# Two fp32 transformer layers on one core: the output-bias column joins the tile of two scalars

## The chip, the cores and the metric

The kernel runs on one core of a Trainium2 chip. The number given is device time in microseconds of one launch, the median of several runs; a profiled execution adds a trace of the engines: PE (TensorE matmuls, with PEld for the loads of their stationary operand), DVE (VectorE), ACT (ScalarE), POOL (GpSimd) and SP (SyncE, which issues nearly all DMAs).

## The reference

One sequence of 2048 rows of width 640 goes through two layers, each a linear-attention block (32 heads of 20) and a squared-ReLU block (hidden width 1728). Both layers use the same weights.

```python
def _A_ref(x, wqkv, wo):                       # linear attention
    q, k, v = split_heads(x @ wqkv)
    phi = lambda t: jnp.where(t > 0, t + 1, jnp.exp(t)) + 1e-6
    pq, pk = phi(q), phi(k)
    kv = einsum("bhsd,bhse->bhde", pk, v)
    den = einsum("bhqd,bhd->bhq", pq, pk.sum over s) + 1e-6
    return (einsum("bhqd,bhde->bhqe", pq, kv) / den) merged @ wo

def _B_ref(x, w1, b1, w2, b2):                 # squared ReLU
    h = x @ w1 + b1
    r = where(h > 0, h, 0)
    return (r * r) @ w2 + b2

x = x + _A_ref(_layernorm(x), A_wqkv, A_wo)    # layer 1
x = x + _B_ref(_layernorm(x), B_w1, B_b1, B_w2, B_b2)
x = x + _A_ref(_layernorm(x), A_wqkv, A_wo)    # layer 2, the same weights
x = x + _B_ref(_layernorm(x), B_w1, B_b1, B_w2, B_b2)
```

## The kernel before

All products are fp32 in three passes: each operand is held as a high and a low half in the matmul format (`R32`), and high x low, low x high and high x high add up in PSUM. The rows are cut into 16 tiles of 128; four of them make a group (`TG`, `GT` = 512 columns).

**The attention half of a layer**, first pass. Tile by tile the rows are normalized, turned and split into `xT`; `part` (its matmuls are at line 574) multiplies them with the weights `kq`, 512, 256 or 320 columns at a time, to give phi(k) and phi(q). The row tiles (`xh`) and phi(k) (`kh`), split, are multiplied into the matrix `G` by `g_part`, also through line 574, 512 columns at a time, three matmuls for each of five PSUM banks. From `G`, the value weights and `wo` a matrix `M` (tiles `uM`) is made for each layer.

**The second half**, group by group: phi(q), divided by its denominator, times `M` (lines 574 and 595), normalization, and then the squared-ReLU block. Its first product is done partly by a Strassen scheme, with 256 columns per matmul (line 1510) and 512 in its rests (line 1520), partly plainly (line 1476, 512 columns). The hidden tiles `h` are split and go into the second product at line 1659 (`fc2_tile`), 512 columns per matmul: for four row tiles the stationary operand is a piece of `h` and the moving one a weight unit `u`, and for the fifth accumulator, the strip of the last 128 output columns, the weight is stationary and `h` moves. The weight units are kept split in DRAM and come back through seven buffers: six of the pool `tmp` (tag `u`, `RING`) and a seventh of the pool of the second half (`ring_tile`, also named `u`). The seventh exists for this half only.

A planner inside the kernel (`Clock`) chooses the order of this half from a table of costs at build time; the recorded order is then fixed, and engines wait for each other by semaphores.

**Where tiles lie.** A tile is a range of bytes in each of the 128 partitions of SBUF. Pools on the left are laid out one after the other from the start, each tile rounded up to 32 bytes: `cpool` (the constants), `small`, `tmp`, and then the pools of a half (`a_` with `G`, `GT`, `acc`, `r`, later `m_` with `uM`). Pools on the right (`ax_` with `xh` and `kh`, later `b_` with `x1`, the seventh `u`, `h` and `hr`) are laid out back from the end.

**The constants around the change.** `scalars` holds -0.5 and 1.0 for each partition; the layer norms raise to the power -0.5 with it (line 530) and one copy makes a tile of ones (line 733). `b2col` holds the last 128 output biases, one per partition. `late_consts` loads it with one DMA of 0.5 KB early in the first pass (line 275), and six copies (line 1668) spread it over a PSUM bank before the strips of the groups.

Of the kernel before, what the change touches and what calls it, by code (L numbers as in the profile page):

```python
# [8 lines left out]
F32 = mybir.dt.float32  # L9
# [4 lines left out]
P = 128  # L14
# [212 lines left out]
def kernel(  # L227
# [15 lines left out]
    cpool = ctx.enter_context(tc.tile_pool(name="cpool", bufs=1))  # L243
# [16 lines left out]

    ident = cpool.tile([P, P], F32, name="ident")
    make_identity(nc, ident)
    scalars = cpool.tile([P, 2], F32, name="scalars")
    neghalf, one = scalars[:, 0:1], scalars[:, 1:2]
    nc.vector.memset(one, 1.0)
    nc.vector.memset(neghalf, -0.5)
    b2bc = cpool.tile([P, D], F32, name="b2bc")
    b2col = cpool.tile([P, 1], F32, name="b2col")
    b1sb = cpool.tile([P, NF], F32, name="b1sb")

    def late_consts():
# [2046 lines left out]
```

## Time and profile before

| | us |
|---|---|
| median of 3 runs | 1376.81 |
| lowest and highest run | 1375.03, 1379.39 |
| the profiled execution | 1382.9 |
| its span, first to last instruction | 1381.2 |

The profiled execution is 6.1 us above the median of the runs, and 1.7 us of it lie outside its span. The mean granted TensorE clock in the span is 0.994 of full speed.

In the views below, a row of the chain of work gives when a piece starts, how long it lasts, the engine, the tile written and the line, and how many instructions make it up. Rows of groups give line, engine, operation, tiles, shape and count, then busy time and mean ns of one, then the idle time before them. Matmuls overlap each other in the pipeline, so the mean time of one is longer than the time from one start to the next; a piece of the chain divided by its count gives the latter.

### The profile page before, as it was taken

How to read it: one execution, taken by the hardware profiler on the slowest of the kernel's cores; microseconds unless marked ns; L12 is line 12 of the kernel's file. 1: busy time of each engine (PE TensorE's matmuls, PEld its weight loads, DVE VectorE, ACT ScalarE, POOL GpSimd, SP SyncE). 2: the span in 40 equal slices, each digit the busy share in tenths (PEclk: the TensorE clock that was granted, in tenths of full speed). 3: DMA queues.
4: the chain of work that ended last, by engine and by line, in shares of the span. 5: the costliest groups of instructions: out<-in, count | busy, mean ns of one | idle time of the engine just before them, and what ended most of it. 6: DMA issues, size and time to landing. Idle time of an engine off the chain costs nothing.

```text
span 1381.2 us, 21322 instructions
## 1 busy us (share of the span) xinstructions
PE 1337.4 (97%) x7616; PEld 1180.7 (85%) x7616; DVE 982.9 (71%) x1928; ACT 770.5 (56%) x1753; POOL 147.2 (11%) x196
## 2 busy tenths in 40 slices
PE   9999989989999999999999999999899999999999
PEld 8888879878888879888888889997788888898887
DVE  8888968887887787354256678799788876874323
ACT  5888845646664655446336687565365644554421
POOL 2334310000000000000012232100000000000000
PEclk9999999999999999999999999999999999999999
DMA  6679685397779768698731114166877788587684
GB/s 200 226 267 333 245 274 181 123 350 240 250 248 307 282 201 307 239 375 306 266 127 44 58 39 132 52 193 229 304 242 221 253 303 265 184 298 273 229 313 175
DMA packets 120240, 316.11 MB, mean 229 GB/s; under 512 B 15110, under 2 KB 40326, under 8 KB 119462
## 3 DMA queue, kind: packets, MB, share of 16 engines
q1 hardware_dynamic: 118622, 312.06, 65.4%
q10 hardware_dynamic: 1512, 2.69, 0.7%
q8 instruction: 60, 0.98, 0.3%
q14 instruction: 46, 0.38, 0.1%
HBM read 251.28 MB, written 64.85 MB: 229 GB/s over the span
## 4 chain that ended last, share of the span: by engine, by line
PE 71%; DMA 12%; DVE 11%; issue 2%; SPq 2%; ACT 1%; POOL 1%; ACTq 0%; DVEq 0%; POOLq 0%
PE PS L574 25%; PE PS L1659 21%; PE PS L1510 15%; PE PS L1520 4%; DMA pqt<-pq 4%; DMA u<-kept_wH 2%; PE PS L1476 2%; DMA u<-kept_w 2%; DMA u<-kept_wG 1%; SPq L773 1%; DMA u<-kept_wE 1%; PE PS L1188 1%; DVE bn L524 1%; DVE uprep L407 1%; PE PS L927 1%
## 5 line engine op out<-in xcount | busy, mean ns | idle before, releaser
L1659 PE MATMUL PS<-u,h 128*128 128x512 f32 x1318 | 346.1, 397 | 1.4 <-ACT s L1532 0.7
L562 ACT ACTIVATE z<-y 32x160 f32<-32x160 f32 x767 | 256.1, 334 | 88.4 <-DVE y L549 69.3
L574 PE MATMUL PS<-kq,xT 128*128 128x320 f32 (+2 forms) x1575 | 283.4, 334 | 4.3 <-DVE r L686 3.5
L1659 PEld LDWEIGHTS PS<-u,h 128*128 128x128 f32 x1318 | 241.1, 190 | 50.3 <-DMA u<-kept_w 1.0
L574 PEld LDWEIGHTS PS<-kq,xT 128*128 128x128 f32 x1575 | 250.0, 188 | 31.5 <-DVE r L686 3.8
L1510 PE MATMUL PS<-tx,u 128*128 128x256 f32 x1152 | 162.7, 284 | 11.1 <-DMA u<-kept_wH 5.9
L1510 PEld LDWEIGHTS PS<-tx,u 128*128 128x128 f32 x1152 | 151.4, 192 | 16.9 <-DMA u<-kept_wH 6.5
L1588 ACT ACTIVATE hr<-PS,b1sb 128x512 f32<-128x512 f32 x104 | 71.2, 685 | 140.9 <-PE PS L1520 123.2
L1510 PEld LDWEIGHTS PS<-xTb,u 128*128 128x128 f32 x864 | 120.5, 189 | 20.1 <-DVE PS L1552 6.8
L1510 PE MATMUL PS<-xTb,u 128*128 128x256 f32 x864 | 127.4, 283 | 7.2 <-DVE PS L1552 4.6
L574 PE MATMUL PS<-kh,xh 128*128 128x512 f32 x480 | 126.9, 398 | 0.0
L529 POOL TENSOR_SCALAR rs<-mv 128x1 f32<-128x1 f32 x62 | 30.5, 492 | 831.0 <-DVE mv L526 831.0
L574 PEld LDWEIGHTS PS<-kh,xh 128*128 128x128 f32 x480 | 88.1, 190 | 15.7
L1594 DVE TENSOR_TENSOR hr<-hr 128x512 f32<-128x512 f32 x71 | 48.7, 687 | 73.6 <-ACT h L1607 73.3
L677 ACT ACTIVATE e<-PS 128x320 f32<-128x320 f32 (+4 forms) x128 | 53.2, 434 | 83.5 <-PE PS L574 71.1
L1607 ACT ACTIVATE h<-hr 128x512 fp32r<-128x512 f32 x104 | 65.0, 629 | 62.3 <-PE PS L1659 61.0
L1659 PE MATMUL PS<-h,u 128*128 128x512 f32 x328 | 94.0, 395 | 0.0
L1597 DVE TENSOR_TENSOR h<-hr,h 128x512 fp32r<-128x512 f32 x104 | 70.9, 685 | 11.4 <-ACT hr L1592 7.4
L685 DVE TENSOR_SCALAR e<-e 128x320 f32<-128x320 f32 (+4 forms) x128 | 41.5, 325 | 50.8 <-ACT e L677 50.3
L1520 PE MATMUL PS<-xTb,u 128*128 128x512 f32 x288 | 76.1, 394 | 0.0
L1659 PEld LDWEIGHTS PS<-h,u 128*128 128x128 f32 x328 | 59.9, 188 | 12.3
L864 POOL TENSOR_TENSOR acc<-acc,r 128x640 f32<-128x640 f32 x28 | 50.7, 1810 | 176.8 <-DVE r L686 176.8
(178 smaller groups left out, 1889.6 us busy)
## 6 DMA issues: line engine op xcount, KB each, us to landing
u<-kept_w SPq DMA_DIRECT2D x116, 640.0 KB, 5.5
u<-kept_wE SPq DMA_DIRECT2D x48, 512.0 KB, 4.3
u<-kept_wH SPq DMA_DIRECT2D x48, 512.0 KB, 5.1
u<-kept_wG SPq DMA_DIRECT2D x48, 512.0 KB, 5.3
u<-kept_wF SPq DMA_DIRECT2D x48, 512.0 KB, 5.2
x<-x SPq DMA_DIRECT2D x48, 320.0 KB, 5.6
pqt<-pq SPq DMA_DIRECT2D x128, 80.0 KB, 5.3
x<-xr SPq DMA_DIRECT2D x32, 320.0 KB, 3.6
```

The costliest lines, as they stand in the source:

```text
L562: nc.scalar.activation(d, v, AF.Copy)
L574: nc.tensor.matmul(ps, a, b, start=first and i == 0, stop=last and i == 2)
L677: nc.scalar.activation(self.e[:, a:b], ps, AF.Exp)
L685: nc.vector.tensor_scalar(e, e, 1.0, PHI_EPS, op0=ALU.min, op1=ALU.add)
L864: nc.gpsimd.tensor_tensor(out=acc, in0=acc, in1=r, op=ALU.add)
L1510: nc.tensor.matmul(ps, l[:, d], r[:, d], start=start and d == 0 and n == 0, stop=d == 1 and n == 2, skip_group_check=True,)
L1520: nc.tensor.matmul(ps, l[:, k], r, start=False, stop=n == 2, skip_group_check=True)
L1588: nc.scalar.activation(r, ps, AF.Relu, bias=b1sb[:, c : c + 1])
L1594: nc.vector.tensor_tensor(out=r, in0=r, in1=r, op=ALU.mult)
L1597: nc.vector.tensor_tensor(out=h[:, 1], in0=r, in1=h[:, 0].bitcast(F32), op=ALU.subtract)
L1607: yield "ACT", cost("ACT", GT), lambda: nc.scalar.activation(h[:, 0], r, AF.Square)
L1659: nc.tensor.matmul(ps, l, r, start=(first or new) and k == 0, stop=end and k == len(a) - 1, **loose)
```

## The change

`b2col` is no longer a tile of its own. The tile `scalars` gets a third column, and the DMA of line 275 writes into that column. A tile of 8 or of 12 bytes takes the same 32, so nothing moves up to `b2bc`; behind it the 32 bytes of `b2col` are gone, and every later tile of the left pools starts 32 bytes nearer to the start of its partition. The right pools stay where they were. The engines' instructions, their order and their waits are the same in both built programs; only addresses differ.

The start bytes in the two built programs, and what is left of them when divided by 64:

| tile (pool) | before | after | by 64, before | by 64, after |
|---|---|---|---|---|
| `ident`, `scalars`, `b2bc` (`cpool`) | 1152, 1664, 1696 | same | 0, 0, 32 | same |
| `b2col` | 4256 | 1672, in `scalars` | 32 | 8 |
| `b1sb` (`cpool`) | 4288 | 4256 | 0 | 32 |
| 12 tiles of tag `f`: `xt`, `st`, `y`, `z`, `pqt`, `xr` and others (`tmp`) | from 5376 | from 5344 | 0 | 32 |
| 2 tiles of tag `T`: `xT`, `xTb` (`tmp`) | 36096, 56576 | 36064, 56544 | 0 | 32 |
| 5 tiles of tag `w`: `kq`, later `tx`, `uT`, `uS` (`tmp`) | from 77056 | from 77024 | 0 | 32 |
| 6 weight units of tag `u` (`tmp`) | from 128256 | from 128224 | 0 | 32 |
| `G`, `uM` (`a_`, `m_`) | from 159616 | from 159584 | 0 | 32 |
| 3 tiles of tag `r`: phi(k), phi(q) (`a_`) | from 175968 | from 175936 | 32 | 0 |
| 8 tiles of tag `x`: `xh`, `kh` (`ax_`) | from 188384 | same | 32 | 32 |
| `x1`, the seventh `u`, `h`, `hr` (`b_`) | 185312, 205792, from 210912, from 223200 | same | 32 | 32 |

The tiles of `tmp` start at a multiple of 256 before and 224 past one after; so do `x1`, the seventh `u`, `xh`, `kh` and `h` in both.

```diff
@@ -260,12 +260,11 @@
 
     ident = cpool.tile([P, P], F32, name="ident")
     make_identity(nc, ident)
-    scalars = cpool.tile([P, 2], F32, name="scalars")
-    neghalf, one = scalars[:, 0:1], scalars[:, 1:2]
+    scalars = cpool.tile([P, 3], F32, name="scalars")
+    neghalf, one, b2col = (scalars[:, i:i + 1] for i in range(3))
     nc.vector.memset(one, 1.0)
     nc.vector.memset(neghalf, -0.5)
     b2bc = cpool.tile([P, D], F32, name="b2bc")
-    b2col = cpool.tile([P, 1], F32, name="b2col")
     b1sb = cpool.tile([P, NF], F32, name="b1sb")
 
     def late_consts():
```

## The prediction

> **What bounds the kernel now.** I read the page's busy times and its chain first, then a table by stage, then the matmuls by shape, and last the chain piece by piece at places where equal matmuls read differently placed tiles. The first two:
>
> ```profile
> PE 1337.4 (97%) x7616; PEld 1180.7 (85%) x7616; DVE 982.9 (71%) x1928; ACT 770.5 (56%) x1753; POOL 147.2 (11%) x196
> ...
> q1 hardware_dynamic: 118622, 312.06, 65.4%
> ...
> PE 71%; DMA 12%; DVE 11%; issue 2%; SPq 2%; ACT 1%; POOL 1%; ACTq 0%; DVEq 0%; POOLq 0%
> ```
>
> TensorE is busy nearly throughout and carries 71% of the chain that ended last; DMA and DVE carry most of the rest. By stage (the middle row is the first pass of layer 2, the rows above and below it the squared-ReLU half of layers 1 and 2, each cut in two; columns: us, busy time and count of PE, PEld, DVE, ACT and POOL, granted clock, DMA share, GB/s):
>
> ```profile
> 262.00:480.00 218.00, 209.51 (x1205) 184.68 (x1205) 176.20 (x350) 121.00 (x264) 8.94 (x16) 0.98 0.79 271
> 480.00:700.00 220.00, 214.58 (x1199) 186.41 (x1198) 114.97 (x223) 104.98 (x238) 7.12 (x17) 0.99 0.78 277
> 700.00:882.00 182.00, 182.00 (x972) 159.63 (x971) 131.40 (x256) 120.14 (x299) 45.79 (x44) 1.00 0.24 74
> 941.00:1160.00 219.00, 207.67 (x1195) 181.66 (x1196) 173.09 (x347) 116.10 (x254) 7.71 (x16) 0.99 0.77 262
> 1160.00:1381.20 221.20, 214.23 (x1213) 186.64 (x1211) 110.86 (x214) 87.46 (x188) 3.55 (x8) 1.00 0.70 250
> ```
>
> From 700 to 882 us PE never stops: there a nanosecond per matmul is a nanosecond of the kernel. In the four other stretches PE stands still 5 to 11 us each, so most, but not all, of a change on PE arrives at the end.
>
> **The change, part by part.** No instruction is added, removed or moved, and no wait either. The column's DMA (0.5 KB, issued at 10.5 us) and its six copies stay; only the byte they touch is another, and it is read 397 us and later. I cost them at nothing:
>
> ```profile
> L1668 ACT ACTIVATE PS<-b2col x6: 594/597/600, 396.9 to 1290.9; 128x512 f32<-128x512 f32 x6
> L275 SPq DMA_DIRECT2D b2col<-in_B_b_dram x1: 328/328/328, 10.5 to 10.5; - x1
> ```
>
> What is left is where tiles lie. I write 0 and 32 for the remainder of a start byte by 64. Before, `tmp` is at 0, and `h`, `kh`, `xh` and the seventh weight buffer at 32; after, all of them are at 32. So the trace of before holds both cases, and the question for each engine is whether its operations cost more or less by it.
>
> *TensorE.* The matmuls that move 512 columns:
>
> ```profile
> L1659 PE MATMUL PS<-u,h 128*128 128x512 f32 x1306 | 344.5, 398 | 1.4 <-ACT s L1532 0.7 <-DMA u<-kept_w 0.7
> L574 PE MATMUL PS<-kq,xT 128*128 128x512 f32 x570 | 136.7, 391 | 0.2 <-DVE GT L716 0.2
> L574 PE MATMUL PS<-kh,xh 128*128 128x512 f32 x480 | 126.9, 398 | 0.0
> L1659 PE MATMUL PS<-h,u 128*128 128x512 f32 x328 | 94.0, 395 | 0.0
> L1520 PE MATMUL PS<-xTb,u 128*128 128x512 f32 x288 | 76.1, 394 | 0.0
> L1476 PE MATMUL PS<-xTb,u 128*128 128x512 f32 x200 | 48.3, 392 | 1.7 <-ACT xTb L286 1.7
> ```
>
> Equal shapes, and yet 391 to 398 ns. By the addresses of the built program, 1,445 of these 3,172 matmuls have one operand at 0 and the other at 32 (I call them mixed): 1,384 of line 1659, where `h` at 32 meets one of the six units at 0, and 36 and 25 of lines 1520 and 1476, where `xTb` at 0 meets the seventh unit. After the change none is mixed. Pieces of the chain show what that is worth. Uniform ones:
>
> ```profile
> 16.68 3.42 PE PS L574 x15
> 352.63 2.05 PE PS L1659 x9
> 382.75 3.42 PE PS L1476 x15
> 1270.07 1.39 PE PS L1520 x6
> 1274.26 2.28 PE PS L1476 x10
> ```
>
> and mixed ones:
>
> ```profile
> 355.36 4.89 PE PS L1659 x21
> 1271.46 2.80 PE PS L1659 x12
> 1276.54 3.50 PE PS L1659 x15
> 1280.03 3.50 PE PS L1476 x15
> ```
>
> Line 1476 is the cleanest pair: 15 matmuls of one kind take 3.42 us (228.0 ns each) where the unit is in a buffer at 0, and 3.50 (233.3) where it is in the seventh. Line 1659 shows it the other way round: with its unit in the seventh buffer, at 32 like `h`, nine take 2.05 (227.8); otherwise 12 take 2.80, 15 take 3.50 and 21 take 4.89 (232.9 to 233.3). So it is not the buffer; it is whether the two operands agree. Nor is it the clock or the load of the DMA engines, for the slower piece had less of the latter (us, PE busy and matmuls touched, clock, DMA share, GB/s):
>
> ```profile
> 1274.26:1276.54 2.28, 2.28 (x11) 1.00 1.01 351
> 1280.03:1283.53 3.50, 3.50 (x16) 1.00 0.57 198
> ```
>
> A uniform run isn't at its best from the start: six that follow 256-column matmuls take 1.39 us, 231.7 each. In the 15 of 3.42 the other nine then take 2.03, 225.6; with the nine of 2.05 beside it (227.8) I take 226.7 once settled. A run of n was 233.3n when mixed and becomes 6 x 231.7 + 226.7(n - 6): 10 ns less for 6, 29 for 9, 49 for 12, 69 for 15. The pieces of this stage hold 6 to 21, most 6 to 12; I take 10, which is 3.6 ns per matmul. The terms:
>
> - 1,445 mixed x 3.6 ns = 5.2 us.
> - 502 uniform ones of lines 1520 and 1659 (252 and 250) stand between mixed ones and rarely settle; 1.5 ns each, 0.8 us.
> - 480 `kh`,`xh` matmuls come in threes and sixes between `kq`,`xT` runs, so the operands agree inside but change over at both ends; they last 398 ns against 391. I take half of these 7 ns: 1.7 us.
> - 570 `kq`,`xT` matmuls meet the same change-over once in 15: about 0.7 ns, 0.4 us.
>
> Sum 8.1 us. The bounds: 2.3 if every run is as short as 6 and nothing else gains (1,445 x 1.6), and 15 if all settle at once (1,445 x 6.6, 502 x 5.0, 480 x 7).
>
> How much arrives: from 700 to 882 all of it. Outside, the chain is on PE for (0.71 x 1381 - 182) / 1199 = 67% of the time; where it is on a DMA, that DMA often waited for a buffer which PE frees, so more than 67% passes. I take 80% of 8.1 = 6.5 us. What is late next is a weight load or the turned phi(q), as at the DMA's 12% today.
>
> The Trainium skill says otherwise ("SBUF — State Buffer", section "A bandwidth-pool intuition that's wrong (but worth ruling out)"): loads of the stationary operand have a second, independent read port, so an engine's two reads shouldn't meet. By that rule the sum would be 0; the pieces of line 1476 above speak against it at 512 columns.
>
> *DVE and ACT.* Splits of 128x512 that read and write tiles at 0, and the same on `h` and `hr` at 32:
>
> ```profile
> L1429 DVE TENSOR_TENSOR tx<-tv,tx 128x512 fp32r<-128x512 f32 x16 | 11.0, 686 | 4.6 <-ACT tx L1427 4.6
> L1597 DVE TENSOR_TENSOR h<-hr,h 128x512 fp32r<-128x512 f32 x104 | 70.9, 685 | 11.4 <-ACT hr L1592 7.4 <-DVE hr L1594 0.5
> L1427 ACT ACTIVATE tx<-tv 128x512 fp32r<-128x512 f32 x16 | 9.9, 625 | 5.8 <-PE PS L1510 4.1 <-DVE tv L1348 1.7
> L1607 ACT ACTIVATE h<-hr 128x512 fp32r<-128x512 f32 x104 | 65.0, 629 | 62.3 <-PE PS L1659 61.0
> ```
>
> 1 ns less and 4 ns more of some 650: nothing. Bounds: 0.2% of DVE's 983 us times its 11% of the chain is 0.2 us either way.
>
> *DMA.* A load of 320 KB into the seventh buffer (224 bytes past a multiple of 256, where all of `tmp` will be) beside the eight of that size into any buffer; stores from `x1`, also at 224, beside stores from a `tmp` tile:
>
> ```profile
> u<-kept_w SPq DMA_DIRECT2D x1, 320.0 KB, 2.9
> u<-kept_w SPq DMA_DIRECT2D x8, 320.0 KB, 3.0
> out_dram<-x SPq DMA_DIRECT2D x14, 320.0 KB, 3.4
> x<-xr SPq DMA_DIRECT2D x32, 320.0 KB, 3.6
> u<-kept_wE SPq DMA_DIRECT2D x48, 512.0 KB, 4.3
> u<-kept_wG SPq DMA_DIRECT2D x48, 512.0 KB, 5.3
> ```
>
> No cost shows: 2.9 against 3.0 and 3.4 against 3.6 us. I take 0. But landings include queueing (the last two rows, of one size, differ by 1.0 us), so up to 10% more per transfer could hide: 10% of the DMA's 12% of the chain, 17 us, is the upper bound; below nothing I see no reason for a gain.
>
> **The sum** against the profiled execution: 1382.9 - 6.5 = 1376.4, its span 1374.7. The runs' median is 6.1 us lower, so 1376.8 - 6.5 = 1370.3 us, 0.47% less. A measurement of this kernel tells about 0.3%, 4.1 us, from no change.
>
> **Rivals.**
>
> 1. *The matmuls get faster and the end doesn't move.* In the four stretches with DMA shares of 0.70 to 0.79 the weights may arrive no sooner, and PE's 5 to 11 us of idle time grows instead. For it: DMA's 12% of the chain. Against it: 182 us without any idle time. Then only the first passes gain (1.7 + 0.4 us) and a third of the 6.0 of the rest: 4.1 us or less, 1373 to 1376.
> 2. *The alignment isn't the cause*, and 228 against 233 follows from something else about which units come when. Then nothing changes: 1376.8. Against it: two lines show it with opposite buffers.
> 3. *Slower: DMA packets cost more at 224 than at 0.* Some 10% per transfer on the chain's DMA, hidden in the spread above, adds 17 and leaves 17 - 6.5 = 10 us more: 1387. It decides for "slower" from 6.4% on ((4.1 + 6.5) / 166). For it: nearly all loads and stores pass through `tmp`. Against it: the 2.9 us landing. The Trainium skill has such a rule ("DMA: Bandwidth & Descriptors", "How a descriptor splits into AXI transactions"): a descriptor that doesn't start at a multiple of 256 bytes costs beats for the bytes before its start, 87 for 80 with 2560 bytes at 224. By it alone my estimate is 9% more for such a packet; the 2.9 us of this trace doesn't agree.
>
> **How the numbers follow.** The forecast, a gain of more than 4.1 us, has 0.74; rival 1 has 0.13, rival 2 0.04; rival 3 0.06, and 0.03 is for a slowdown that I don't see, on POOL or in the queues. Faster is 0.74, same 0.17, slower 0.09. For the range, the likeliest case alone spans 8.1 x 0.67 to the middle of 8.1 and 15, all arriving: 5.4 to 11.5 us, 1365 to 1371. With rivals 1 and 2, and the runs' own 2 us to each side, it reaches from 1364 to 1379; that leaves out rival 3 and the far end of the gain.
>
> **What would show it.** Right: line 1659's `u,h` matmuls fall from 398 ns towards 392 to 394, line 1476's 25 in the seventh buffer to 228.0 per start, and the stretch 700 to 882 shortens by about 1 us; line 1510's 256-column matmuls stay at 283. Rival 1: the same, but more idle PE time before lines 1510 and 574. Rival 2: 398 stays. Rival 3: the DMA queue's 65.4% rises by 3 points or more, and the median landings with it. The prediction is wrong above all if short runs hardly settle (the 1.6 ns bound), or if some engine that I saw as indifferent minds `r` and `tmp` changing sides.

## The result and the profile after

The changed kernel takes 1378.02 us (median of 12 runs, 1373.96 to 1386.07); the kernel before takes 1379.68 on the same chip. The ratio is 0.9997, 95% interval 0.9975 to 1.0019: no difference that can be told. The forecast was 1370.3 us against a median of 1376.81, a ratio of 0.9953; that median was of three runs, 2.9 us below the one of twelve.

The page of the changed kernel has these three rows for those shown first (busy times, the main DMA queue, the chain). All lines behind the edit carry a number smaller by one.

```profile
PE 1334.1 (97%) x7616; PEld 1184.6 (86%) x7616; DVE 982.4 (71%) x1928; ACT 771.0 (56%) x1753; POOL 147.1 (11%) x196
...
q1 hardware_dynamic: 118622, 312.06, 66.6%
...
PE 70%; DMA 12%; DVE 11%; issue 2%; SPq 2%; ACT 2%; POOL 1%; ACTq 0%; DVEq 0%; POOLq 0%
```

PE is busy 3.3 us less. Its span is 1380.1 us, 1.1 shorter, so PE's idle time (span less busy) has grown from 43.8 to 46.0 us. The DMA queue moves the same packets and bytes and is busy for 1.2 points more.

The matmuls of the changed kernel by shape (busy us, mean ns of one):

```profile
L1658 PE MATMUL PS<-u,h 128*128 128x512 f32 x1306 | 338.8, 393 | 2.2 <-ACT PS L1665 0.7 <-ACT s L1531 0.7 <-DMA u<-kept_w 0.7
L1509 PE MATMUL PS<-tx,u 128*128 128x256 f32 x1152 | 164.5, 286 | 10.5 <-DMA u<-kept_wG 4.6 <-DMA u<-kept_wH 3.9 <-ACT s L1531 1.5
L573 PE MATMUL PS<-kq,xT 128*128 128x512 f32 x570 | 135.5, 390 | 0.2 <-DVE GT L715 0.2
L573 PE MATMUL PS<-kh,xh 128*128 128x512 f32 x480 | 125.3, 394 | 0.0
L1658 PE MATMUL PS<-h,u 128*128 128x512 f32 x328 | 93.0, 392 | 0.0
L1519 PE MATMUL PS<-xTb,u 128*128 128x512 f32 x288 | 77.8, 400 | 0.0
```

The matmuls with 512 columns are faster in every group but the last, in which some fell into stretches of half clock (below). The 256-column ones of line 1509 (1510 before) are at 286 instead of 284 ns. The chain at the place that the prediction used:

```profile
1270.86 2.72 PE PS L1658 x12
1273.58 2.27 PE PS L1475 x10
1275.85 3.40 PE PS L1658 x15
1279.25 3.40 PE PS L1475 x15
```

The 12 that took 2.80 us take 2.72, and the two 15s, at 3.50 before, take 3.40 (226.7 ns each). The ten that were uniform already take 2.27 for 2.28. By stage (same columns as before):

```profile
262.00:480.00 218.00, 209.52 (x1204) 185.09 (x1204) 175.51 (x350) 120.98 (x263) 8.94 (x16) 0.98 0.81 273
700.00:882.00 182.00, 182.00 (x979) 160.74 (x978) 133.28 (x259) 122.44 (x304) 45.81 (x44) 1.00 0.24 74
941.00:1160.00 219.00, 203.40 (x1181) 179.28 (x1180) 170.35 (x341) 113.86 (x250) 7.71 (x16) 0.99 0.79 262
```

In the 182 us without idle time PE now starts 979 matmuls where it started 972. From 941 to 1160 us it does less than before (1181 for 1195, busy 203.40 for 207.67 us): there it waits, at a DMA share that rose from 0.77 to 0.79 for the same 262 GB/s.

To add this up I took from the trace, for each matmul, the time to the start of the next, less what a settled run of its size needs: 226.7 ns at 512 columns and 120.0 at 256, as measured in these traces, and for other sizes the line through the two (146.7 at 320). The excess, summed (us):

| | 512 columns | 256 columns | waits (over 25 ns each) | in stretches of half clock |
|---|---|---|---|---|
| before | 14.7 | -3.0 | 64.2 | 8.5 |
| after | 7.2 | -1.6 | 65.4 | 12.4 |

So the gain came almost as sized: 7.5 us at 512 columns where 8.1 were forecast, of which 1.4 are lost again at 256 columns (u64 and midpad show why). Some 6.1 us are left, and yet the end moved by 1.1. The clock took 3.9 in this one execution. Whether that, the waits or a loss elsewhere takes the gain in all the runs is what the experiments ask.

### The profile page after: what moved, and what is told of

It reads as the page before. It is cut to its first block, busy times and chain, and to the rows that moved or that the text cites. A ratio compares the mean times of both kernels' runs of the same rounds, so it can differ in the third digit from the quotient of the medians.

```text
span 1380.1 us, 21322 instructions
## 1 busy us (share of the span) xinstructions
PE 1334.1 (97%) x7616; PEld 1184.6 (86%) x7616; DVE 982.4 (71%) x1928; ACT 771.0 (56%) x1753; POOL 147.1 (11%) x196
## 4 chain that ended last, share of the span: by engine, by line
PE 70%; DMA 12%; DVE 11%; issue 2%; SPq 2%; ACT 2%; POOL 1%; ACTq 0%; DVEq 0%; POOLq 0%
PE PS L573 25%; PE PS L1658 21%; PE PS L1509 15%; DMA pqt<-pq 4%; PE PS L1519 4%; PE PS L1475 3%; DMA u<-kept_wH 1%; DMA u<-kept_wG 1%; SPq L772 1%; DMA st<-in_B_w_dram 1%; DVE bn L523 1%; PE PS L1187 1%; DVE uprep L406 1%; PE PS L926 1%; DMA kept_wH<-uprep 1%
## 5 line engine op out<-in xcount | busy, mean ns | idle before, releaser
L1658 PE MATMUL PS<-u,h 128*128 128x512 f32 x1318 | 340.4, 392 | 2.2 <-ACT PS L1665 0.7
L573 PEld LDWEIGHTS PS<-kh,xh 128*128 128x128 f32 x480 | 87.6, 189 | 14.8
L1541 DVE TENSOR_TENSOR PS<-PS,s 128x256 f32<-128x256 f32 x48 | 20.8, 432 | 71.0 <-ACT PS L1537 71.0
```

The lines of the kernel that those rows point to most:

```text
L573: nc.tensor.matmul(ps, a, b, start=first and i == 0, stop=last and i == 2)
L1658: nc.tensor.matmul(ps, l, r, start=(first or new) and k == 0, stop=end and k == len(a) - 1, **loose)
```

## The experiments

All kernels here have the same instructions in the same order and differ only in where tiles lie (tiles may have other names). Each got 12 timed runs beside 35 of the kernel before on the same chip; the four kernels of a round share these 35. The two theories: the matmuls' gain is real and the twelve `f` tiles, which left multiples of 256, cost as much on the DMA side; or the gain is real and the end doesn't follow, because PE then waits for its weights. A third, that it is not the agreement of the operands at all, is what the first four test. In the expectations of the last four runs the theories are numbered: 1 is the first of these, 2 the second.

The table has all results. PE idle is span less busy time, both from the page; the 512-column excess is worked out as above; the last column is the mean time of the main queue's packets of 640 bytes (16,384 of them, the loads `pqt<-pq` of 80 KB). PE idle, excess and packets come from one profiled execution each.

| run | `f` tiles, past a multiple of 256 | ratio, 95% interval | PE busy | PE idle | excess at 512 | 640-byte packet, ns |
|---|---|---|---|---|---|---|
| before | 0 | | 1337.4 | 43.8 | 14.7 | 43.9 |
| right0 | 0 | 0.9973, 0.9957 to 0.9990 | 1331.2 | 42.8 | 11.2 | 42.0 |
| all0 | 0 | 0.9970, 0.9956 to 0.9985 | 1330.3 | 44.1 | 7.2 | 43.2 |
| all0_b | 0 | 0.9963, 0.9945 to 0.9981 | 1330.5 | 41.3 | 7.1 | 43.7 |
| afterf0 | 0 | 0.9987, 0.9966 to 1.0007 | 1330.3 | 45.3 | 7.2 | 44.5 |
| u64 | 0 | 0.9998, 0.9982 to 1.0015 | 1332.3 | 48.1 | 16.3 | 43.6 |
| midpad | 0 | 1.0025, 1.0007 to 1.0044 | 1339.0 | 42.9 | 15.0 | 43.8 |
| after | 224 | 0.9997, 0.9975 to 1.0019 | 1334.1 | 46.0 | 7.2 | 47.8 |
| again | 224 | 1.0011, 0.9993 to 1.0029 | 1331.7 | 47.5 | 7.1 | 46.0 |
| again_b | 224 | 1.0001, 0.9979 to 1.0023 | 1334.5 | 50.9 | 7.1 | 48.0 |
| shift32 | 32 | 1.0021, 1.0005 to 1.0036 | 1334.2 | 47.6 | 11.1 | 46.7 |
| shift64 | 64 | 1.0035, 1.0017 to 1.0053 | 1337.0 | 43.4 | 15.6 | 46.1 |
| f192 | 192 | 1.0016, 0.9998 to 1.0034 | 1335.4 | 46.8 | 14.8 | 46.2 |
| f224 | 224 | 1.0024, 1.0007 to 1.0041 | 1338.3 | 48.0 | 14.6 | 46.3 |

### The change again, and the same agreement in other ways

The changed kernel, unedited:

> The changed kernel once more. Theory A (operands that agree by 64 bytes save TensorE about 7.6 us of matmul starts; the trace of the changed kernel shows that 3.9 us of it were lost to stretches at half clock, 1.4 us to 256-column matmuls that had been catching up, 1.2 us to longer waits): against the kernel before on the same chip 0.2 to 0.4% less at equal granted clock; over many runs 0.1 to 0.4% less, since the half-clock stretches fall as they like. Theory B (half clock comes with the denser matmuls): the granted clock is lower than before by some 0.002 to 0.003 in most runs, and the time the same within 0.1%. DMA queue share 66 to 67% of the span against 65.4 before.

1381.85 us, ratio 1.0011. The median is on the other side of 1, the interval still holds it: no difference. The mean granted clock of these runs is 0.9920 beside 0.9941 for the kernel before, the sign that theory B named; all0, below, speaks against it.

An unused tile of 32 bytes moves the left pools 32 bytes on instead of back:

```diff
     b1sb = cpool.tile([P, NF], F32, name="b1sb")
+    cpool.tile([P, 8], F32, name="pad")
```

> The kernel before with one unused tile of 32 bytes behind the bias tile, so that the left pools lie 32 bytes further on instead of 32 nearer: start bytes at 32 by 64, and 32 instead of 224 by 256. Theory A: the same matmul pattern as the changed kernel, line of the second product 392 to 393 ns instead of 398, time 0.1 to 0.4% less than before. If agreement by 256 counts, not by 64: the matmuls stay at 398, time as before. For the DMA: if the cost of 640- and 2560-byte packets in the changed kernel (47.8 and 123.6 ns against 43.9 and 120.0) comes with any start off 256, it shows here too; if it grows with the bytes before the start, it is nearly gone.

1384.42 us, ratio 1.0021: slower, where theory A expected faster. The operands are now all at 32 by 64, but the left ones at 32 by 256 and the right ones at 224. The excess at 512 columns falls to 11.1, half of what the change takes off.

The same with 64 bytes (`[P, 16]`), after which operands are mixed as before:

> Control: the kernel before with an unused tile of 64 bytes, so that the left pools keep their remainder by 64 (0) and lose that by 256 (64). Theory A: matmuls exactly as before (398 and 398 ns in the two mixed groups, 1,445 mixed), time within 0.2% of before, or up to 0.2% more if the DMA's packets mind a start off 256. If any shift from before changes the pattern: the matmuls change here too.

1386.84 us, ratio 1.0035. No gain on the matmuls (15.6), and the largest loss of all, more than the 0.2% allowed for. So something that isn't on PE minds where the left pools lie.

Only the right pools move, by 32 bytes; the left ones, and with them the `f` tiles, stay at multiples of 256:

```diff
     cpool = ctx.enter_context(tc.tile_pool(name="cpool", bufs=1))
+    rpool = ctx.enter_context(tc.tile_pool(name="rpool", bufs=1, side="right"))
+    rpool.tile([P, 8], F32, name="rpad")
```

> The left pools as before, at 0 by 64 and 0 by 256; instead the right pools lie 32 bytes nearer to the start (an unused tile of 32 bytes at their end), so that h, kh, xh and the seventh weight buffer are at 0 by 64 as well. Theory A: all operands agree at 0, matmuls as in the changed kernel (392 to 393 ns), packets of the left pools as before (43.9 and 120.0 ns), time 0.25 to 0.45% less than before and 0.05 to 0.2% less than the changed kernel. If it is 32 that is fast, not agreement: matmuls slower than before, time 0.3% more.

1376.49 us, ratio 0.9973: faster, though its agreement is that of shift32 (0 by 64; 0 and 192 by 256) and its excess too (11.2). By shape:

```profile
L1661 PE MATMUL PS<-u,h 128*128 128x512 f32 x1306 | 340.0, 394 | 1.9 <-DMA u<-kept_w 1.3 <-ACT su L1849 0.6
L576 PE MATMUL PS<-kh,xh 128*128 128x512 f32 x480 | 127.1, 398 | 0.0
```

With the same gain at 512 columns, one kernel ends 0.27% earlier and the other 0.21% later. This already speaks against waits for weights that eat any gain, and for a loss in the left pools. In the rows above `u,h` falls from 398 ns to 394, and `kh,xh` stays at 398.

### Everything at 0, and single tiles off 0

All matmul operands and all `f` tiles at multiples of 256: the right pools 224 bytes nearer to the start, and three small tiles of the layer norm in one, which brings `tmp` to 5120.

```diff
+    rpool = ctx.enter_context(tc.tile_pool(name="rpool", bufs=1, side="right"))
+    rpool.tile([P, 56], F32, name="rpad")
...
-        st = small.tile([P, 2, 6], F32, tag="bn", name="bn")
+        ln = small.tile([P, 16], F32, tag="bn", name="bn")
+        st = ln[:, :12].rearrange("p (a b) -> p a b", a=2)
...
-        mv = small.tile([P, 2], F32, tag="mv", name="mv")
+        mv = ln[:, 12:14]
...
-        rs = small.tile([P, 1], F32, tag="rs", name="rs")
+        rs = ln[:, 14:15]
```

> All matmul operands and all DMA buffers at a multiple of 256 at once: the right pools 224 bytes nearer to the start (an unused tile at their end), and the three small tiles of the layer norm merged into one, so that the left pools lie 256 bytes nearer to the start and make room. Theory C (the changed kernel has two effects: matmuls save 6 us because their operands agree, and about 4 us come back because DMA buffers of the pool tmp no longer start at multiples of 256): matmuls settle as in the changed kernel (excess over the settled rate of the 512-column matmuls 7 us, against 14.7 before and 11.2 with the right pools at 192), 640-byte packets 42 to 44 ns, time 0.35 to 0.5% less than before. Rival (nothing is lost to DMA buffers, the matmul gain is simply absorbed): time within 0.2% of before, like the changed kernel.

1376.94 us, ratio 0.9970, with the same excess at 512 columns as the changed kernel (7.2). Once more on another chip:

> The version with every operand of the matmuls and every f tile at a multiple of 256, a second time on another chip. Both theories: ratio 0.9955 to 0.998; a ratio above 0.999 would mean that the first result belonged to one chip.

1376.50 us, ratio 0.9963. Its page:

```profile
PE 1330.5 (97%) x7616; PEld 1183.3 (86%) x7616; DVE 982.5 (72%) x1928; ACT 770.9 (56%) x1753; POOL 147.1 (11%) x196
```

With a span of 1371.8 us PE is idle for 41.3: faster matmuls don't make PE wait more.

Only the `f` tiles (and the small ones) off 256, by 192; the column of hidden biases moves behind them:

```diff
-    b1sb = cpool.tile([P, NF], F32, name="b1sb")
...
+            b1sb = tmp.tile([P, NF], F32, tag="b1", name="b1sb", bufs=1)
```

> Only the twelve tiles of tag f leave the multiples of 256: b1sb (64 bytes) goes behind them in the pool tmp, so they start at 192 by 256 and 0 by 64; weights, xT, kq and all matmul operands stay where they were. Theory C, with the loss in the f tiles (rows of 2560 and 640 bytes, phi(q) among them): 0.2 to 0.35% more than before, 640-byte packets 46 ns and more. If the loss is in the weight units: time as before.

1382.87 us, ratio 1.0016, interval 0.9998 to 1.0034: slower by 0.16%, which by itself is just not shown. PE's matmuls are as before (14.8), the 640-byte packets take 46.2 for 43.9 ns.

Only what lies behind the tiles of tag `w` moves, by 64 bytes: the weight units, `G`, `uM` and `r`.

```diff
-        return tmp.tile([P, 4 * D], R32, tag="w", name=name, bufs=DC)
+        t = tmp.tile([P, 4 * D], R32, tag="w", name=name, bufs=DC)
+        if not upad:
+            upad.append(tmp.tile([P, 16], F32, tag="pad", name="pad", bufs=1))
+        return t
```

> Only the six weight units (and the pools behind them) leave the multiples of 256: an unused tile of 64 bytes between kq and the units, which start at 64 by 256. Theory C with the loss in the f tiles: time within 0.1% of before. If the loss is in the weight units, on whose landing the matmuls wait: 0.2 to 0.35% more, and longer landings of the units.

1380.30 us, ratio 0.9998. The loads of weight units, most of the bytes, don't mind leaving a multiple of 256. The packets' time is unmoved. For the matmuls the run shows two more things. All six units in `tmp` are now 64 bytes past a multiple of 256, while `tx` and `xTb` lie at one, so these operands agree by 64 and not by 256:

```profile
L1481 PE MATMUL PS<-xTb,u 128*128 128x512 f32 x200 | 49.0, 395 | 1.7 <-ACT xTb L286 1.7
L1515 PE MATMUL PS<-tx,u 128*128 128x256 f32 x1152 | 159.6, 281 | 13.6 <-DMA u<-kept_wH 6.9 <-DMA u<-kept_wG 4.6 <-ACT s L1537 1.5
```

At 512 columns (line 1476 before) they are slower for it, 395 ns where they were 392: agreement by 64 alone gained nothing here. At 256 columns (line 1510 before) they are faster, 281 where they were 284, an excess of -8.0 us for -3.0. That is why PE's busy time is low here.

32 bytes between the `T` tiles (`xT`, `xTb`) and the `w` and `u` tiles behind them, so that other matmuls agree and disagree, with the `f` tiles in place:

```diff
                 T4[0] = tmp.tile([P, TG, 2, D], R32, tag="T", name="xT", bufs=2)
+                tmp.tile([P, 8], F32, tag="pad", name="pad", bufs=1)
```

> An unused tile of 32 bytes between xT and kq in the pool tmp: f tiles and xT, xTb stay at 0, kq, the weight units and the pools behind are at 32. The mixing then changes sides: the second product (units and h at 32) becomes uniform, and kq with xT, 570 matmuls of 512 columns, and all of lines 1476 and 1520 become mixed. By agreement: the stretch of the first pass that is TensorE alone (182 us, 240 matmuls of kq and xT) gets 1.0 to 1.6 us longer, kq,xT matmuls go from 391 to 396 or more, the second product from 398 to about 394. If only a weight or a hidden tile at 32 matters: kq,xT stay at 391. Time within 0.3% of before; the DMA of the units at 32 by 256 may add to it.

1384.10 us, ratio 1.0025. The sides change as the agreement would have it: `kq` at 32 now meets `xT` at 0, and `u` at 32 meets `xTb` at 0,

```profile
L574 PE MATMUL PS<-kq,xT 128*128 128x512 f32 x570 | 139.0, 395 | 0.2 <-DVE GT L716 0.2
L1477 PE MATMUL PS<-xTb,u 128*128 128x512 f32 x200 | 49.0, 396 | 1.6 <-ACT xTb L286 1.6
```

395 ns where it was 391, and 396 where it was 392, while `u` with `h` falls from 398 to 396. With another line and other buffers slow, it is the agreement and not the buffer, the line or the order. At 256 columns `kq` with `xT` is faster where the two disagree, as in u64: 116.6 ns from start to start, behind six or more of the same tiles, for 119.2 before and 120.0 in the changed kernel. As a time it is a slower kernel than its excess (15.0) explains, and its `f` tiles are in place, so a loss of this size can come about without them. Part of it is the clock (a mean of 0.9927 over its runs, where the kernel before has 0.9942); the rest stays open.

### The change in two parts

First the constants and the `f` tiles move as in the change, and 32 bytes behind the `f` tiles put all the rest of the left pools back (edits against the changed kernel):

```diff
             a_load(0, src)
+            tmp.tile([P, 8], F32, tag="pad", name="pad", bufs=1)
```

> One part alone: the column joins the scalars as in the change, but 32 bytes left free behind the twelve f tiles put everything behind them back where it was. Only the f tiles and the constants move to 224 past a multiple of 256; the matmuls are mixed as before. Theory 1 (the f tiles eat what the matmuls gain): +2.5 to +5 us, ratio 1.002 to 1.0035; the 640-byte packets go from 44 to 46 to 48 ns, and the accounting of the 512-column matmuls stays near 14.7 us. Theory 2 (the f tiles are innocent, the gain is lost in waits on the weights): within 1.5 us, ratio 0.999 to 1.001.

1384.15 us, ratio 1.0024, interval 1.0007 to 1.0041.

```profile
PE 1338.3 (97%) x7616; PEld 1181.9 (85%) x7616; DVE 982.7 (71%) x1928; ACT 770.9 (56%) x1753; POOL 147.2 (11%) x196
...
L1659 PE MATMUL PS<-u,h 128*128 128x512 f32 x1306 | 345.2, 398 | 0.4 <-DMA u<-kept_w 0.4
```

The matmuls are as before, DVE and ACT too (to 0.4 us of their sums), and the kernel is slower. This part of the change is a loss.

Then the matmul tiles move as in the change, and the `f` tiles stay at a multiple of 256. The layer norm's tiles are merged as in all0, and two tiles fill up:

```diff
     b1sb = cpool.tile([P, NF], F32, name="b1sb")
+    cpool.tile([P, 8], F32, name="cpad")
...
             a_load(0, src)
+            tmp.tile([P, 56], F32, tag="pad", name="pad", bufs=1)
```

> The other part alone: matmul operands lie where the change puts them, but the f tiles stay at multiples of 256: the layer norm's three small tiles become one, 32 bytes are left free behind the constants, which puts the f tiles at 5120, and 224 bytes behind the f tiles. Theory 1: the gain of the matmuls arrives, -3.5 to -6.5 us, ratio 0.9955 to 0.9975, with 512-column matmuls at 7.2 us of excess and 640-byte packets near 44 ns. Theory 2: as the change itself, ratio 0.999 to 1.001.

1380.75 us, ratio 0.9987, interval 0.9966 to 1.0007.

```profile
PE 1330.3 (97%) x7616; PEld 1182.0 (86%) x7616; DVE 982.3 (71%) x1928; ACT 770.8 (56%) x1753; POOL 147.1 (11%) x196
```

PE is busy 7.1 us less than before, as in all0. The ratio lies between the two theories and its interval holds both, so this run alone decides nothing; its median is 1.1 us below that of the changed kernel beside it:

> The changed kernel once more, beside the two that part it, on the same chip. Theory 1: the sum of the two parts, ratio 0.998 to 1.001. Theory 2: the same as the kernel with the f tiles put back. A ratio of 0.9965 or less would mean that neither loss exists and the earlier intervals were unlucky.

1381.88 us, ratio 1.0001. The changed kernel shows no gain in any of three measurements (0.9997, 1.0011, 1.0001).

### What the table says together

Of the kernels whose 512-column matmuls gained, the four measurements with the `f` tiles at a multiple of 256 have ratios of 0.9963 to 0.9987 (right0, all0, all0_b, afterf0), and the four with them off it 0.9997 to 1.0021 (after, again, again_b, shift32). Without that gain, off it is 1.0016 to 1.0035 (f192, f224, shift64), in place 0.9998 (u64) and 1.0025 (midpad, which doesn't fit).

In the traces the loss shows as idle time of PE. With the `f` tiles in place it is 44.0 us on average (seven executions, 41.3 to 48.1), off it 47.2 (seven, 43.4 to 50.9): 3.1 us more. One of each kind is on the wrong side; for off it that is shift64, whose time rose most, so its loss isn't seen in its trace. The part of it that DVE ended is 21.4 us on average in place and 24.4 off it, which is nearly all of the difference. DVE's own wait for the `pqt` loads (line 784, `pr`) is 21.7 us (18.9 to 23.9) and 24.9 (23.6 to 26.4), 3.3 more. The 640-byte packets part the two kinds without overlap: 42.0 to 44.5 ns in place, 46.0 to 48.0 off it.

PE's busy time is 1337.0 us on average where the operands are mixed as before (before, f192, f224) and 1331.9 where they agree by 256 (after, again, again_b, all0, all0_b, afterf0): 5.1 us less. The excess gives 6.1; the busy time also holds the half clock, and the clock of the second group's executions is lower (0.9927 for 0.9937). Where the matmuls gained and the `f` tiles stayed (right0, all0, all0_b, afterf0), PE is idle for 41.3 to 45.3 us, about the 43.8 of before.

The clock differs between the kernels' runs too: its mean is 0.9929 over the 36 runs of the changed kernel and 0.9940 over the 105 of the one before. Within the runs of one kernel a thousandth goes with about 1.1 us (slope over all 261). With the clock taken off so, the mean of afterf0 is 3.0 us below the kernel before (95%: 1.3 to each side) and that of again_b, beside it, 0.3 (1.6); f192 is 2.7 above (1.3), f224 1.4 (1.5) and midpad 1.6 (1.6). So at equal clock the `f` tiles are worth 1.4 to 2.7 us in these comparisons.

For the change this makes -6.1 us on PE, +3.1 in waits and +1.2 by the clock: -1.8 us, or 0.9987. That lies inside the first and the third interval of the changed kernel and just below the second (0.9993), so up to 2 us stay unexplained. The lower clock doesn't follow from denser matmuls: all0 and all0_b stand as densely and had 0.9943 and 0.9937, where the kernel before beside them had 0.9942 and 0.9936. It may come from the waits themselves (last section): the seven sets of runs with `f` tiles off 256 had 0.9930 on average, the seven others 0.9937. This leans that way and shows no more.

That `f` tiles off 256 cost time is shown by f224 against the kernel before (f192 leans the same way) and by the two groups with the matmuls' gain. That the slower packets are the way by which they do it is argued: DVE's longer wait for `pqt` fits it, DVE's and ACT's own work is unmoved, and no kernel slowed these packets without moving the `f` tiles.

## Why the prediction was wrong

**Right: nothing but addresses.** Instructions, packets and bytes are the same in number.

**Right: the matmuls at 512 columns, nearly to the size.** By terms, in excess per group: `u`,`h` and `h`,`u` lost 5.0 us (9.2 to 4.2), where the mixed and the uniform ones of line 1659 were put at 5.0 + 0.4; lines 1520 and 1476 lost 0.4 of 0.6 forecast; `kh`,`xh` 0.9 of 1.7; `kq`,`xT` 1.2 instead of 0.4. The last two misses cancel, which is luck. The runs settle at 226.7 ns, as taken. The signs that were named are there: 398 falls to 393 ns (392 to 394 forecast), and the 182 us do seven more matmuls, about 1 us. Line 1475's starts settle lower than the 228.0 named. What "agree" means was only half seen: the prediction counted by 64. Agreement by 64 alone gave half of the gain in right0 and shift32 (14.7 to 11.2), whose operands are 192 apart by 256, and none in u64, where `xTb` and `u` are 64 apart. It is agreement by 256 that gives all of it, and that the change brings it is luck: 224 happened to be the remainder on the right.

**Missed: the 256-column matmuls.** They were to stay at 283 ns and rose from 284 to 286, 1.4 us. At this size it is the operands that disagree by 256 that go faster: behind six or more of the same tiles, 115.7 ns from start to start in u64 (`tx` with `u`) and 116.6 in midpad (`kq` with `xT`), for 120.0 in the changed kernel. So the change, which makes all agree, had to lose a little here.

**Not refuted: the share that arrives, 80%.** all0 has the matmul gain of the change (7.5 - 1.4 = 6.1 us by excess) and ends 0.30 and 0.37% earlier, 4.1 and 5.1 us: 67 and 84%. afterf0 has it too and ends only 0.13% earlier, 1.8 us, though its interval reaches to 0.34%. Rival 1 would have had PE's idle time grow with the gain, and it doesn't where the `f` tiles stay; its upper end of 4.1 us, though, is still inside these intervals. In the changed kernel idle time did grow, for the other reason.

**Failed: "No cost shows ... I take 0" of the DMA.** The rows beneath it compared `u` tiles with a `u` tile, and stores from `x1`. The unit loads indeed cost nothing (u64). But the tiles of tag `f` are another kind of buffer, with loads of 80 KB in rows of 640 bytes, and no row of before showed one of these tiles off a multiple of 256. For these the packets rose by 7% (43.5 to 46.7 ns, means of the seven executions of each kind), those of 2560 bytes by 2% (120.2 to 122.3), those of 4096 and 5120 bytes by about 1% or less in the changed kernel (313.8 to 315.4 and 255.8 to 258.5 us over the 16 engines). In PE's idle time the `f` tiles show as 3.1 us, and f224, where only the `f` tiles and the constants have moved, ends 3.3 us later: half of the 6.1 us that the matmuls saved. With the clock's 1.2 us it leaves 1.8 of them, too little to be told from no change. The upper bound of 17 us covered the cost; the value taken did not. That 1378.02 us lies inside the stated 1364 to 1379 is luck: the range was laid around a three-run median 2.9 us below that of twelve runs.

**Rival 3 was right in kind and wrong in size.** It asked for 3 points on the queue; there were 1.2 in this execution and 0.4 to 0.5 in the other two of the same kernel. Of the median landings `pqt<-pq` and `x<-xr` rose a little:

```profile
pqt<-pq SPq DMA_DIRECT2D x128, 80.0 KB, 5.6
x<-xr SPq DMA_DIRECT2D x32, 320.0 KB, 3.8
```

Landings are too coarse to see it: in u64, with all `f` tiles in place, the first is 5.6 as well. Only the packets' own times part the kernels. The rule of the Trainium skill named there ("DMA: Bandwidth & Descriptors", "How a descriptor splits into AXI transactions") agrees in sign, for the short packets. It would give 9% at 2560 bytes and 224, where the four runs at 224 show 1 to 3% (121.9 to 123.6 for 120.2 ns), though not all packets of this size touch a tile that moved. The four rows of a `pqt` tile lie 640 bytes apart, so that in a tile at a multiple of 256 every second one starts 128 past it. Counted by rows, my estimate from the rule is 5, 9, 9 and 14% more at 32, 64, 192 and 224, where the runs gave 7, 6, 6 and 6 to 10% (46.7, 46.1, 46.2 and 46.0 to 48.0 ns for 43.5).

**DVE and ACT, 0.** Right: 982.4 and 771.0 us for 982.9 and 770.5.

## What to carry to other kernels

Where tiles lie is a setting of its own: an edit that frees 32 bytes moves every tile behind it, and with them the speed of matmuls and of DMAs, in opposite directions if one is unlucky. In this kernel it paid to put the moving and the stationary operand of 512-column matmuls at the same remainder by 256 (at 256 columns a different one), and the tiles that short-row DMAs fill at multiples of 256; the version that does both (all0) is 0.3 to 0.4% faster than either kernel here. When a neutral resource is costed by a row of the trace, it must be a row of the same buffers and the same packet size, not of the largest transfers.

## What the runs showed of the hardware

- A run of fp32r matmuls with 512 columns goes at 226.7 ns where the start bytes of both operands agree by 256 (changed kernel), and at 233.3 where they lie at 0 and 224 by 256 (before, line 1476 with the seventh unit) or at 0 and 64 (u64, `xTb` with `u`). With 0 and 192 (right0) or 32 and 224 (shift32) `u` with `h` settles at 230.3. At 256 columns it is the other way round: 120.0 ns where they agree, 115.7 at 0 and 64 (u64) and 116.6 at 32 and 0 (midpad). At 320 columns there was no difference (an excess of 0.0 to -0.4 us over some 1,800 matmuls in every kernel). Moving all tiles together by 224 changes nothing: 7.2 in after and in all0. The Trainium skill ("SBUF — State Buffer", "A bandwidth-pool intuition that's wrong (but worth ruling out)") has the two reads independent of each other, and these runs don't agree with it at 512 columns.
- The granted clock drops to half in stretches of 3.41 us or two or three of them in a row. In the 14 profiled executions there are 66 such stretches (three to six in each, without the last microseconds), and in each execution all of them start on one grid of 3.413 us, to 1 ns. In the grid's step before each stretch PE was idle for 1.68 us or more of its 3.41; no step with more than 1.87 us of idle time was without a stretch behind it (some 5,500 steps). So a wait of about 2 us costs a second time, about 1.7 us of lost clock, if it falls into one step, and nothing more if the grid cuts it in two. The Trainium skill ("TensorE: Matmul & The Clock Gate", "Part 1: The HAM clock gate (the "warmup" mystery)") has the free-running window of 3.413 us, and these traces agree with it; it takes an idle window for the clock to fall, where here half of one was enough. Where the grid lies against the program differs between executions, which makes it a source of the spread between runs: five stretches are 0.6% of the span at half speed, the 0.994 of the page. In the changed kernel's profiled execution one wait, at 289 us, was followed by three steps in a row, which is most of the 3.9 us that the clock cost there.
